# One expert's second weights and w_in change places between attention and the expert stage, and hash bits are written by one instruction and transfers

## The chip, the cores and the metric

The kernel runs on one core of a Trainium2 chip. The metric is the device time of one execution in microseconds. Before the change it is 560.36 us, the median of three runs (559.76 to 561.38). All figures of the profile come from one more execution that was profiled.

## The reference

Three layers follow each other, on float32 inputs of 2 x 8 heads x 768 tokens x 64:

```python
# 1. attention between tokens of the same hash
q_bits = (einsum(q, proj) > 0); k_bits = (einsum(k, proj) > 0)     # 6 bits each
mask = bucket(q_bits)[:, None] == bucket(k_bits)[None, :]
attn = softmax(where(mask, q @ k.T / 8, -1e9)) @ v                 # -> x, 1536 x 512
# 2. mixture of 8 experts, each token to the one of its largest logit
e = argmax(x @ w_gate)
x = gate * sigmoid(x @ w_output_gate)[e] * (relu(x @ w1[e]) @ w2[e])   # 512 -> 1024 -> 512
# 3. h = x @ w_in (512 -> 1024); solu = h * softmax(h); layer norm; @ w_out (1024 -> 512)
```

w_in and w_out come as 64-bit floats, all else as 32-bit.

## The kernel before

**Numbers in halves.** TensorE multiplies 16-bit floats. A 32-bit matrix is split into a high half (the value rounded to 16 bits) and a low half (the rest), and three products (high-high, high-low, low-high) are added. So every weight has to be loaded, scaled, rounded (`w_hi`, L141, on ScalarE) and subtracted (`w_lo`, L144, on VectorE), or split by three POOL instructions (`w_split`, L179). An expert's w1 or w2 comes in four loads of 512 KB (`w_load`, L152) into tiles of the pool `raw`, which has five buffers, used in turn: a new tile waits until the one five places earlier has been read. w_in and w_out, being 64 bits wide, come in eight pieces each of 128 x 512 values (`wide_load`, L101) into five buffers `raww`. A piece is decoded to 32-bit floats: ScalarE takes Abs of its upper word (L122), VectorE shifts and joins the words in three steps (L123, L125, L126; `wide_a`) and sets small values to zero in a fourth (L131; `wide_b`), and then `w_hi` and `w_lo` split it.

**Attention** (`attention`, L281) works on 96 units: eight pairs of heads, two blocks of queries, two heads, three tiles of 128 queries. The loop over units (L938) issues for unit i: the scores of 128 queries against 768 keys (`emit_s`, L530, four products), between them the transposes of unit i-2's probabilities (L577), the row maximum on VectorE (L548), the exponential on ScalarE (L563), a part of the product with v, and what was put into a list for this unit by `at(i, f, ...)`. That list, written out by hand (L874 to L906), is where all other work is placed: splitting and transposing the next pair's q and k, hash bits, the routing of tokens to experts, the zero fill of the row buffer xs (`zero`, L273), and the loads and POOL splits of w1 and w2 of experts 0 and 1 (`pieces`, L902: 16 loads). Twelve units, one pair of heads, are called a period here; its units are counted from 0.

The mask is not applied but added: the operands `c` and `b` hold the hash bits as large values, and the second product of `emit_s` adds them to the scores. A product (`bits_mm`, L489) gives the sums whose signs are the bits, four groups of 32 rows for two heads and two halves of the tokens, in one PSUM tile; `bits_rows` (L506) compares one group of 32 rows x 384 columns and writes it to 32 other rows of `c` or `b`. So there are four VectorE instructions for q and four for k in each of seven periods, spread over units 5, 6, 9, 10 and 11 of the period ahead (`BITS`, L874).

Every engine runs its instructions in the order in which they are issued. SyncE's queue carries nearly all transfers, in one order too: a transfer whose tile is not free holds those behind it.

**The seam** (L961 to L1160) ends attention, routes the last tokens, sorts the experts by their token counts and starts the expert stage. Three wide pieces are loaded there, then `x_load(1)` (L1033), a transposing transfer of the rows of the second expert, which waits until all tokens are scattered to xs, then the next weights and two more pieces.

**The expert stage** is a list of 64 slots (L1165), four for each expert's first layer (`mm1`) and four for its second (`mm2`), in the order m1 0, m1 1, m2 0, m1 2, m2 1, m1 3, ... m2 6, m2 7. A slot holds 24 products. `prep` (L1166) says which weight load is rounded in which slot (its low half follows in the next, its load goes out three slots ahead); slots 4 to 47 and 52 to 55 have one. `WD` (L1186) gives the slot in which the decoding of each of the 16 wide pieces begins. After an `mm2` pair, ScalarE writes the high half of yT and VectorE the low half (L1145, L1146); the latter is issued a slot later (`run_late`) and frees the PSUM buffer, one of four that both layers take in turn.

The last stage multiplies by w_in (L1260), applies the activation and the norm, and multiplies by w_out (L1325).

Of the kernel before, what the change touches and what calls it, by code (L numbers as in the profile page):

```python
# [21 lines left out]
def kernel(  # L22
# [77 lines left out]

    def wide_load(x, dec, t=None):  # L101
        if t is None:
            t = dec.tile([128, 512, 2], I32, tag="raww", name="raww", bufs=5)
# [11 lines left out]
    def wide_a(x, dec):  # L115

        t = wide_t.pop(x)
        hi, lo = t[:, :, 1], t[:, :, 0]
        d = nc.vector
        b = dec.tile([128, 512], I32, tag="db", name="db")  # L120
        m = dec.tile([128, 512], F32, tag="dm", name="dm", bufs=1)
        nc.scalar.activation(out=m, in_=hi, func=AF.Abs)  # L122
        d.tensor_scalar(out=b, in0=hi, scalar1=0x07FFFFFF, scalar2=3, op0=ALU.bitwise_and,  # L123
                        op1=ALU.logical_shift_left)
        d.scalar_tensor_tensor(out=b, in0=lo, scalar=29, in1=b, op0=ALU.logical_shift_right, op1=ALU.bitwise_or)  # L125
        d.scalar_tensor_tensor(out=b, in0=hi, scalar=-0x40000000, in1=b, op0=ALU.bitwise_and, op1=ALU.bitwise_or)  # L126
        dec_t[x] = b.bitcast(F32), m
# [12 lines left out]

    def w_hi(src, dst, c0, scale):  # L141
# [6 lines left out]
    wt = {}  # L148
    rawq = {}
# [17 lines left out]
    def w_args(name, e, c):  # L167
# [6 lines left out]
        if c == 0 and (name, e) not in wt:  # L174
            tag = "wb" if name == "w2" else "wa"
            wt[name, e] = wp.tile([128, 2, 4096], F16, tag=tag, name=tag)
# [104 lines left out]
    def attention(es):  # L281
# [232 lines left out]
        bt_ = {}  # L514
# [353 lines left out]
        def gather_copy():  # L868
            xw = raw.tile([128, 1024], F32, tag="raw", name="raw").bitcast(F16)[:, 0:8 * CAP]
            xw = gx["xw"] = xw.rearrange("p (c n) -> p c n", c=8)  # L870
            for kk in range(4):
                nc.scalar.copy(out=xw[:, kk::4], in_=gx["ps"][kk][:, 0:2 * CAP].rearrange("p (a n) -> p a n", a=2))

        BITS = (((5, "q"), (0, 1)), ((6, "q"), (2, 3)),  # L874
                ((9, "k"), (0,)), ((10, "k"), (1, 2)), ((11, "k"), (3,)))
        for n in range(1, NP):
# [8 lines left out]
            for x, gs in BITS:  # L885
                at(s0 + x[0], bits, n, x[1], gs)
# [13 lines left out]
        for e in range(E):  # L900
            at(8 + 4 * e, zero, e)
        pieces = [(nm, e, c) for e in range(2) for nm in ("w1", "w2") for c in range(4)]  # L902
        for x, pc in enumerate(pieces):
            s0 = 12 * (x // 2) + ((10 if x % 2 else 4) if x < 14 else (5 if x % 2 else 1))
# [19 lines left out]
    with tc.manual_schedule():  # L924
# [90 lines left out]
        PRE = 5 if wide else 0  # L1015
        if wide:
# [361 lines left out]
```

## Time and profile before

| | |
|---|---|
| time of the profiled execution | 559.89 us |
| its span, first to last instruction | 558.0 us |
| TensorE (PE) busy | 516.1 us, 92% |
| VectorE (DVE) busy | 422.0 us, 76% |
| ScalarE (ACT) busy | 341.1 us, 61% |
| POOL busy | 260.2 us, 47% |
| mean granted TensorE clock | 0.995 |
| moved by DMA | 81.74 MB |

The stages, from the starts of their first matmuls: attention 9.43 to some 254, the seam to 267.69, the expert stage to 422.28, the last stage to 558.0. Slot 24 of the expert stage begins at 331.27, slot 32 at 351.07, slot 40 at 373.91, slot 48 at 392.84.

Of the rows below, a timeline row gives the start, the length, the engine ("SPq" is SyncE's queue), the line, the operation, the tiles written and read, their sizes, and in brackets the idle time before it and what ended it. A row of a group by lines gives the count, the total busy time and the mean length in ns. A waits row gives the total, the number and the longest. A windows row gives start and end, the length, each engine's busy time and instructions (PE, PEld for TensorE's weight loads, DVE, ACT, POOL), the granted TensorE clock, the DMA engines' busy share and the GB/s moved; length less busy time is idle time.

### The profile page before, as it was taken

How to read it: one execution, taken by the hardware profiler on the slowest of the kernel's cores; microseconds unless marked ns; L12 is line 12 of the kernel's file. 1: busy time of each engine (PE TensorE's matmuls, PEld its weight loads, DVE VectorE, ACT ScalarE, POOL GpSimd, SP SyncE). 2: the span in 40 equal slices, each digit the busy share in tenths (PEclk: the TensorE clock that was granted, in tenths of full speed). 3: DMA queues.
4: the chain of work that ended last, by engine and by line, in shares of the span. 5: the costliest groups of instructions: out<-in, count | busy, mean ns of one | idle time of the engine just before them, and what ended most of it. 6: DMA issues, size and time to landing. Idle time of an engine off the chain costs nothing. (4 is left out here: it accounts for less than half of the span.)

```text
span 558.0 us, 10766 instructions
## 1 busy us (share of the span) xinstructions
PE 516.1 (92%) x3900; PEld 348.8 (63%) x3900; DVE 422.0 (76%) x935; ACT 341.1 (61%) x642; POOL 260.2 (47%) x324
## 2 busy tenths in 40 slices
PE   6799999999899999999997988968999999999994
PEld 5455656656555555667997988968995444444441
DVE  7877878788888898757699899889981875455540
ACT  6678687777767777764376776776661554244240
POOL 7959483838587674625247556331330111111112
PEclk9999999999999999999999999989999999999999
DMA  5576758453819166003687999999700252423442
GB/s 169 113 227 106 252 87 273 85 175 62 256 32 220 67 137 174 2 1 117 220 239 172 282 286 275 236 336 303 264 4 2 38 95 58 113 56 66 105 82 70
DMA packets 104488, 81.74 MB, mean 146 GB/s; under 512 B 79728, under 2 KB 86768, under 8 KB 104432
## 3 DMA queue, kind: packets, MB, share of 16 engines
q1 hardware_dynamic: 102128, 74.71, 51.8%
q0 software_dynamic: 2304, 6.31, 3.1%
q8 instruction: 32, 0.52, 0.4%
q14 instruction: 24, 0.20, 0.1%
HBM read 51.43 MB, written 9.97 MB: 110 GB/s over the span
## 5 line engine op out<-in xcount | busy, mean ns | idle before, releaser
L563 ACT ACTIVATE p<-s,mx 128x768 f32<-128x768 f32 x96 | 95.2, 992 | 56.3 <-DVE mx L552 46.9
L577 PE MATMUL t<-ident,p 128*128 128x128 f32 x576 | 125.4, 274 | 0.9 <-ACT pt L579 0.6
L548 DVE TENSOR_REDUCE mx<-s 128x1 f32<-128x768 f32 x96 | 91.6, 954 | 24.2 <-PE s L538 21.6
L579 ACT COPY pt<-t 128x384 f32<-128x384 f32 x192 | 84.5, 478 | 10.1 <-PE t L577 8.8
L577 PEld LDWEIGHTS t<-ident,p 128*128 128x128 f32 x576 | 78.0, 141 | 15.9 <-ACT pt L579 7.0
L596 PE MATMUL v<-pt,v 128*64 128x384 f32 (+1 forms) x384 | 80.1, 503 | 2.9 <-DVE xt L623 2.5
L1116 POOL TENSOR_TENSOR hh<-hf,hh 128x448 f16<-128x448 f32 (+5 forms) x32 | 42.9, 1346 | 79.6 <-ACT hf L1115 70.4
L1105 PE MATMUL a<-xw,wa 128*128 128x224 f16 (+5 forms) x224 | 55.8, 253 | 15.9 <-DVE yT L1146 14.8
L1325 PE MATMUL o<-wo,zT 128*128 128x512 f16 x288 | 64.0, 379 | 2.1 <-DMA zT<-z 2.1
L1260 PE MATMUL h<-wi,yT 128*128 128x512 f16 x288 | 64.0, 380 | 1.2 <-ACTq L1065 0.6
L1136 PE MATMUL a<-hh,wb 128*128 128x224 f16 (+5 forms) x256 | 63.5, 251 | 0.0
L1137 PE MATMUL a<-hh,wb 128*128 128x224 f16 (+5 forms) x256 | 63.5, 251 | 0.0
L1138 PE MATMUL a<-hh,wb 128*128 128x224 f16 (+5 forms) x256 | 63.5, 251 | 0.0
L538 PE MATMUL s<-k,q 128*128 128x384 f16 x192 | 58.7, 330 | 4.0 <-ACT p L563 4.0
L538 PE MATMUL s<-b,cm 128*128 128x384 f16 x192 | 57.3, 326 | 1.1 <-DVE b L510 1.1
L1107 PE MATMUL a<-xw,wa 128*128 128x224 f16 (+5 forms) x224 | 55.9, 253 | 1.5 <-DVE wa L146 1.5
L1106 PE MATMUL a<-xw,wa 128*128 128x224 f16 (+5 forms) x224 | 55.9, 253 | 0.0
L1325 PEld LDWEIGHTS <-zT 128*128 128x128 f16 x288 | 27.9, 98 | 36.8 <-DMA zT<-z 3.6
L1260 PEld LDWEIGHTS <-yT 128*128 128x128 f16 x288 | 27.9, 98 | 35.7 <-issue 0.9
L538 PEld LDWEIGHTS <-q 128*128 128x128 f16 x192 | 19.4, 101 | 39.5 <-issue 37.7
L1275 ACT ACTIVATE ex<-h,st,csc 128x1024 f32<-128x1024 f32 x12 | 14.4, 1203 | 45.8 <-DVE st L1298 34.5
L1272 DVE TENSOR_REDUCE st<-h 128x1 f32<-128x1024 f32 x12 | 14.7, 1224 | 31.9 <-PE h L1260 31.9
(256 smaller groups left out, 1038.4 us busy)
## 6 DMA issues: line engine op xcount, KB each, us to landing
raw<-in_moe_w_dram SPq DMA_DIRECT2D x64, 512.0 KB, 6.2
raww<-in_moe_w_in_dram SPq DMA_DIRECT2D x8, 512.0 KB, 8.2
raww<-in_moe_w_out_dram SPq DMA_DIRECT2D x8, 512.0 KB, 6.2
xs<-raw SPq DMA_DIRECT2D x8, 448.0 KB, 6.9
v<-in_v_dram SPq DMA_DIRECT2D x8, 384.0 KB, 5.5
q<-in_q_dram SPq DMA_DIRECT2D x7, 384.0 KB, 4.7
k<-in_k_dram SPq DMA_DIRECT2D x7, 384.0 KB, 5.8
cm<-q SPq DMA_DIRECT2D x14, 96.0 KB, 2.1
```

What stands on the lines that cost most here:

```text
L538: nc.tensor.matmul(t[:, c, 0:SB], d[x, h][:, s], flat(d[y, h])[:, c * SB:(c + 1) * SB], start=first, stop=not first)
L548: nc.vector.tensor_reduce(out=mx[:, 0:1], in_=t[:, :, 0:SB], op=ALU.max, axis=AX.XY)
L563: nc.scalar.activation(out=p, in_=s_t.pop(i)[:, :, 0:SB], func=AF.Exp, scale=mx[:, 1:2], bias=mx[:, 2:3], accum_out=sums[j][:, qt, h:h + 1])
L577: nc.tensor.transpose(t[:, g * 128:(g + 1) * 128], p[:, c, g * 128:(g + 1) * 128], ident)
L579: nc.scalar.copy(out=pt[j, h][:, 3 * c:3 * c + 3, qt * 128:(qt + 1) * 128], in_=t[:, 0:SB].rearrange("p (g c) -> p g c", g=3))
L596: nc.tensor.matmul(pv[j, q0][64 * h:64 * h + 64, 0:w], vt[:, h, c], pt[j, h][:, c, q0 * 128:q1 * 128], start=(c == 0), stop=(c == NS - 1), ...
L1106: nc.tensor.matmul(ps[:, i, 0:n], w[:, 0, kk, fs], xw[:, KD + kk], start=False, stop=False)
L1136: nc.tensor.matmul(ps, w[:, 0, f, ds], hh[:, 0, f], start=(f == 0), stop=False)
L1137: nc.tensor.matmul(ps, w[:, 0, f, ds], hh[:, 1, f], start=False, stop=False)
L1138: nc.tensor.matmul(ps, w[:, 1, f, ds], hh[:, 0, f], start=False, stop=(f == KF - 1))
L1260: nc.tensor.matmul(ps[:, c], yT[:, a, kk, ts], w_i[:, w, kk, c * 512:(c + 1) * 512], start=(kk == 0 and a == 0 and w == 0), stop=(kk == KD ...
L1325: nc.tensor.matmul(ps, zT[:, KF * a + f], w_o[:, w, f], start=(f == 0 and a == 0 and w == 0), stop=(f == KF - 1 and a == 1))
```

## The change

Three things change.

Pieces of w_in (eight) are loaded and decoded during attention into the tile `wi`, one piece every 11 units from unit 6 on: load four units ahead into a `raw` tile, Abs and the first VectorE step in unit u, the other three in u+1 to u+3, `w_hi` on ScalarE in u+4, and the low half on POOL in u+5 (two instructions, `wide_lo_pool`). In their place w2 of expert 1 is no longer loaded and split in attention: `pieces` has 12 loads instead of 16. Its tile now lies in the pool `yp`, which begins after attention.

At the seam, w2 of expert 1 is loaded (two loads ahead of `x_load(1)`, the others behind) and split in slots 0 to 4 by ScalarE and VectorE. Of the wide pieces only the eight of w_out are left for the expert stage; `WD` begins them in slots 2, 5, 8, 11, 14, 20, 26 and 32.

Hash bits of a pair: one VectorE instruction on 128 partitions writes all four groups into a `raw` tile, and four transfers on SyncE's queue take the groups to their rows; units 5 and 9 of the period hold them. The zero fill of xs goes out in units 9 to 16 instead of every fourth unit from 8 to 36.

```diff
@@ wide_a, now in three steps, with raw tiles when dec is None
-        t = wide_t.pop(x)
+        for step in range(3):
+            wide_s(x, dec, step)
+    def wide_s(x, dec, step):
+        t = wide_t[x]
...
+            if dec is None:
+                bm = raw_t()
+                b, m = bm[:, 0:512], bm[:, 512:1024].bitcast(F32)
...
+    def wide_lo_pool(x):
+        src, dst, c0, scale = wide_parts(x)
+        hi, lo = (dst[:, a, c0:c0 + 512] for a in range(2))
+        nc.gpsimd.tensor_scalar(out=src, in0=src, scalar1=scale, scalar2=1.0, op0=ALU.mult, op1=ALU.mult)
+        nc.gpsimd.tensor_tensor(out=lo, in0=src, in1=hi, op=ALU.subtract)
@@ attention
-        def bits(n, which, gs):
-            if 0 in gs:
-                bt_[n, which] = ps_m.tile([128, 512], F32, tag="m", name="m")
-                bits_mm(n, which, range(4), bt_[n, which])
-            for g in gs:
-                bits_rows(n, which, g, bt_[n, which])
+        def bits(n, which):
+            m = ps_m.tile([128, 512], F32, tag="m", name="m")
+            bits_mm(n, which, range(4), m)
+            x, i, val, cmp = ("c", 0, MASK, ALU.is_ge) if which == "q" else ("b", 1, -MASK, ALU.is_le)
+            t = raw.tile([128, 1024], F32, tag="raw", name="raw").bitcast(F16)[:, 0:SB]
+            nc.vector.tensor_scalar(out=t, in0=m[:, 0:SB], scalar1=thr[:, i:i + 1], scalar2=val, op0=cmp, op1=ALU.mult)
+            for g in range(4):
+                h, blk = divmod(g, 2)
+                r = slice(64 - 64 * h, 96 - 64 * h)
+                nc.sync.dma_start(out=flat(op[n][x, h])[r, blk * SB:(blk + 1) * SB], in_=t[32 * g:32 * g + 32])
...
-        BITS = (((5, "q"), (0, 1)), ((6, "q"), (2, 3)),
-                ((9, "k"), (0,)), ((10, "k"), (1, 2)), ((11, "k"), (3,)))
+        BITS = ((5, "q"), (9, "k"))
...
-            at(8 + 4 * e, zero, e)
-        pieces = [(nm, e, c) for e in range(2) for nm in ("w1", "w2") for c in range(4)]
+            at(9 + e, zero, e)
+        pieces = [(nm, e, c) for nm, e in (("w1", 0), ("w2", 0), ("w1", 1)) for c in range(4)]
+        wt["wi", 0] = wp.tile([128, 2, 4096], F16, tag="wi", name="wi", bufs=1)
+        for x in range(2 * KD if wide else 0):
+            u = 6 + 11 * x
+            at(u - 4, wide_load, x, None)
+            for step in range(3):
+                at(u + step, wide_s, x, None, step)
+            at(u + 3, wide_b, x)
+            at(u + 4, lambda x: w_hi(*wide_parts(x)), x)
+            at(u + 5, wide_lo_pool, x)
@@ seam and expert stage
+        for c in range(2):
+            w_load("w2", 1, c)
         x_load(1, slice(NT, NT + CAP))
...
-        prep = [None] * 4
+        prep = [("w2", 1, c) for c in range(4)]
...
-        WD = [0, 2, 4, 6, 8] + [14 + 4 * x for x in range(11)]
+        WD = [2, 5, 8, 11, 14, 20, 26, 32]
...
-        for x in range(4, 4 + LA):
-            if prep[x]:
-                w_load(*prep[x])
+        for x in range(2, LA):
+            w_load(*prep[x])
+        expert(2)
```

## Rows read from the trace of the kernel before

**Rows 1.** Windows: three kinds of attention period, and the expert stage in two parts.

```profile
98.53:128.55 30.02, 29.90 (x206) 18.09 (x205) 24.21 (x57) 22.73 (x49) 19.41 (x23) 1.00 0.49 121
128.55:160.26 31.71, 30.00 (x210) 18.18 (x209) 26.86 (x71) 22.80 (x49) 23.18 (x29) 1.00 0.53 140
160.26:192.30 32.04, 30.19 (x210) 18.27 (x208) 27.65 (x71) 22.61 (x49) 22.85 (x28) 1.00 0.57 139
192.30:222.78 30.48, 30.39 (x207) 18.07 (x205) 27.49 (x71) 22.84 (x53) 19.32 (x22) 1.00 0.59 142
...
267.69:331.27 63.58, 55.70 (x577) 54.64 (x577) 56.61 (x99) 41.78 (x73) 31.57 (x30) 1.00 0.83 236
331.27:392.84 61.57, 52.11 (x578) 51.14 (x577) 56.32 (x63) 43.23 (x67) 23.03 (x21) 0.97 1.02 286
```

**Rows 2.** Windows: the expert stage by eight slots, from slot 24 on.

```profile
331.27:351.07 19.80, 17.75 (x194) 17.45 (x193) 19.15 (x21) 13.78 (x21) 11.06 (x12) 1.00 1.12 264
351.07:373.91 22.84, 18.20 (x194) 17.81 (x193) 18.38 (x23) 15.48 (x25) 5.91 (x5) 0.93 0.97 288
373.91:392.84 18.93, 16.16 (x195) 15.87 (x193) 18.79 (x21) 13.97 (x23) 6.05 (x6) 1.00 0.96 308
```

**Rows 3.** Waits of TensorE, 267 to 393 us.

```profile
PE a L1105 <- DVE yT L1146: 14.8, 9, 4.6
```

**Rows 4.** Groups by line of VectorE, 267 to 408 us.

```profile
L146 DVE SCALAR_TENSOR_TENSOR wb<-raw,wb 128x1024 f16<-128x1024 f32 x22 | 32.5, 1482 | 0.0
L146 DVE SCALAR_TENSOR_TENSOR wa<-raw,wa 128x1024 f16<-128x1024 f32 x24 | 30.0, 1249 | 0.0
L126 DVE SCALAR_TENSOR_TENSOR db<-raww,db 128x512 int32<-128x512 int32 x15 | 13.1, 872 | 0.5
...
L123 DVE TENSOR_SCALAR db<-raww 128x512 int32<-128x512 int32 x15 | 8.6, 570 | 10.9 <-DMA raww<-in_moe_w_out_dram 4.8 <-issue 3.3 <-DMA raww<-in_moe_w_in_dram 2.8
...
L146 DVE SCALAR_TENSOR_TENSOR wo<-db,g,wo 128x512 f16<-128x512 f32 x7 | 7.8, 1116 | 0.0
```

**Rows 5.** Timeline of VectorE in the expert stage.

```profile
276.33 0.43 DVE L123 TENSOR_SCALAR db<-raww 128x512 int32<-128x512 int32 x1 [3.25 <-issue]
...
280.91 0.69 DVE L125 SCALAR_TENSOR_TENSOR db<-raww,db 128x512 int32<-128x512 int32 x1
...
328.42 0.62 DVE L1146 SCALAR_TENSOR_TENSOR yT<-a,yT 128x448 f32 x1
```

**Rows 6.** Waits of SyncE's queue, whole span.

```profile
SPq L1035 <- DMA xs<-xh,slot_all: 8.0, 1, 8.0
```

**Rows 7.** Groups by line of ScalarE, 267 to 408 us.

```profile
L122 ACT ACTIVATE dm<-raww 128x512 f32<-128x512 int32 x15 | 10.2, 678 | 9.5 <-DMA raww<-in_moe_w_in_dram 3.5 <-DMA raww<-in_moe_w_out_dram 3.2 <-issue 2.7
```

**Rows 8.** Timeline of VectorE and POOL in attention, around 149 us.

```profile
148.55 2.13 POOL L184 TENSOR_TENSOR wa<-raw,wa 128x1024 f16<-128x1024 f32 x1
...
149.03 0.17 DVE L745 TENSOR_REDUCE hn<-oh_all 128x8 f16<-128x24 f16 x1
...
149.23 1.47 DVE L746 TENSOR_TENSOR hs<-hs,hn 128x8 f16<-128x8 f16 x1
```

**Rows 9.** Windows: two attention units, the first a period's unit 1, the second its unit 0.

```profile
70.72:73.16 2.44, 2.43 (x17) 1.33 (x15) 1.71 (x4) 2.19 (x6) 2.36 (x3) 1.00 0.18 36
160.26:162.47 2.21, 2.21 (x17) 1.33 (x15) 2.08 (x5) 1.32 (x4) 2.04 (x5) 1.00 0.00 0
```

**Rows 10.** Timeline: key bits of a pair, and the product that reads them first.

```profile
64.28 0.61 DVE L510 TENSOR_SCALAR b<-m,thr 32x384 f16<-32x384 f32 x1 [0.45 <-PE m L504]
...
69.07 0.33 PE L538 MATMUL s<-b,cm 128*128 128x384 f16 x1
```

**Rows 11.** DMA issues by line: KB each, median us to landing.

```profile
raw<-in_moe_w_dram SPq DMA_DIRECT2D x64, 512.0 KB, 6.2
...
cm<-q SPq DMA_DIRECT2D x14, 96.0 KB, 2.1
```

**Rows 12.** Timeline of SyncE's queue: an issue that waits for nothing.

```profile
181.97 0.47 SPq L158 DMA_DIRECT2D raw<-in_moe_w_dram  x1
```

More of the change, by code (lines that the diff above doesn't have):

```diff
@@ L99, with raw_t @@
     wide_t = {}
+    def raw_t():
+        return raw.tile([128, 1024], F32, tag="raw", name="raw").bitcast(I32)
     def wide_load(x, dec, t=None):
-        if t is None:
+        if dec is None:
+            t = raw_t().rearrange("p (c t) -> p c t", t=2)
+        elif t is None:
             t = dec.tile([128, 512, 2], I32, tag="raww", name="raww", bufs=5)
@@ L115, in wide_a @@
     def wide_a(x, dec):
-        t = wide_t.pop(x)
+        for step in range(3):
+            wide_s(x, dec, step)
+    def wide_s(x, dec, step):
+        t = wide_t[x]
         hi, lo = t[:, :, 1], t[:, :, 0]
         d = nc.vector
[L120 to L127, printed above, removed]
+        if step == 0:
+            if dec is None:
+                bm = raw_t()
+                b, m = bm[:, 0:512], bm[:, 512:1024].bitcast(F32)
+            else:
+                b = dec.tile([128, 512], I32, tag="db", name="db")
+                m = dec.tile([128, 512], F32, tag="dm", name="dm", bufs=1)
+            dec_t[x] = b.bitcast(F32), m
+            nc.scalar.activation(out=m, in_=hi, func=AF.Abs)
+            d.tensor_scalar(out=b, in0=hi, scalar1=0x07FFFFFF, scalar2=3, op0=ALU.bitwise_and,
+                            op1=ALU.logical_shift_left)
+            return
+        b = dec_t[x][0].bitcast(I32)
+        if step == 1:
+            d.scalar_tensor_tensor(out=b, in0=lo, scalar=29, in1=b, op0=ALU.logical_shift_right, op1=ALU.bitwise_or)
+        else:
+            d.scalar_tensor_tensor(out=b, in0=hi, scalar=-0x40000000, in1=b, op0=ALU.bitwise_and, op1=ALU.bitwise_or)
     def wide_b(x):
@@ L148 @@
     wt = {}
+    w2p = [wp, None]
     rawq = {}
@@ L174, in w_args @@
         if c == 0 and (name, e) not in wt:
-            tag = "wb" if name == "w2" else "wa"
-            wt[name, e] = wp.tile([128, 2, 4096], F16, tag=tag, name=tag)
+            if name == "w1":
+                wt[name, e] = wp.tile([128, 2, 4096], F16, tag="wa", name="wa")
+            else:
+                wt[name, e] = (w2p[e % 2] or wp).tile([128, 2, 4096], F16, tag=f"wb{e % 2}", name="wb", bufs=1)
         return [(t, wt[name, e], c * 1024, W_S)]
@@ L884, in attention @@
                 at(s0 + 20, load, n + 1, "v")
-            for x, gs in BITS:
-                at(s0 + x[0], bits, n, x[1], gs)
+            for x, which in BITS:
+                at(s0 + x, bits, n, which)
         for j in range(2 * NP):
@@ L1026 @@
         mp = moe.enter_context(tc.tile_pool(name="mp", bufs=2, reuse_waits="tile"))
-        for nm in ("wi", "wo"):
-            wt[nm, 0] = yp.tile([128, 2, 4096], F16, name=nm)
+        w2p[1] = yp
+        wt["wo", 0] = yp.tile([128, 2, 4096], F16, name="wo")
         yT = yp.tile([128, 2, KD, NT + CAP], F16, name="yT")
@@ L1184, in each @@
                 f(*a)
-        WD = [0, 2, 4, 6, 8] + [14 + 4 * x for x in range(11)]
-        for x in range(16):
-            i = WD[x] if wide else 3 + 3 * x
+        WD = [2, 5, 8, 11, 14, 20, 26, 32]
+        for x in range(W0 if wide else 0, 16):
+            i = WD[x - W0] if wide else 3 + 3 * x
             if wide:
-                if x >= PRE:
+                if x >= W0 + PRE:
                     put(i - 3, wide_load, x, dec)
@@ L1210 @@
                 each(w_lo, prep[i - 1])
-            if 4 <= i < len(prep) - LA and prep[i + LA]:
+            if i < len(prep) - LA and prep[i + LA]:
                 w_load(*prep[i + LA])
```

13 lines of the change are left out of this document (6 added, 7 removed).

## The prediction

> **What bounds the kernel now.** I read the page first: it gives TensorE 92% of the span and VectorE 76%, so on the average TensorE bounds. The average hides where it does not, so next came the windows by stage, with TensorE's idle time as length less busy time. In attention a period of 12 units (one head pair) lasts 30.0 us with TensorE busy 29.9 [rows 1]: TensorE sets its pace, and VectorE (24.2 us) and ScalarE (22.7 us) fit beside it. The expert stage, 267.69 to 422.28, is different: TensorE is idle 7.9 us up to 331.27 and 9.5 us from there to 392.84, while VectorE is busy 56 us in each half [rows 1]. Cut by eight matmul slots (four of a second layer, four of a first), VectorE works 19.15 of 19.80 us and 18.79 of 18.93 us; in the stretch between, with 18.38 of 22.84 us, it had to wait for loads itself [rows 2]. The waits say who is late: TensorE waits 14.8 us for yT of L1146, the low half that VectorE writes and that frees a PSUM buffer, and next to nothing else [rows 3]. So the expert stage runs at VectorE's pace, with DMA close behind (286 GB/s at a busy share of 1.02) [rows 1].
>
> In the third view, the groups by line, VectorE's work there is: low halves of the expert weights at 1.25 us (w1) and 1.48 us (w2), and per w_in or w_out piece four decoding steps of 0.57, 0.75, 0.87 and 0.85 us (the first and the third stand for the four) and 1.12 us for the low half of w_out [rows 4], 4.2 us for one of 16 pieces.
>
> **The change part by part.**
>
> *Expert stage from 331.27 to 392.84 (slots 24 to 47).* Before, about six pieces were decoded there; in the changed order, with a piece begun at slots 2, 5, 8, 11, 14, 20, 26 and 32, only the pieces of 26 and 32 and the end of that of 20 remain. VectorE then needs 12 x 1.48 + 12 x 1.25 + 6 x 0.6 (yT) + 2 x 4.2 + 1.1 = 45.8 us, where it was busy 56.3. TensorE needs 50.5 us: 52.1 busy less the 1.6 (0.07 x 22.84) that a mean granted clock of 0.93 of the full 2.4 GHz cost in the stretch that also holds its longest wait, 4.6 us [rows 1 to 3]. So VectorE is no longer last, and what comes last is TensorE or DMA. DMA moved 0.286 x 61.6 = 17.6 MB; about five and a half loads of 512 KB go, leaving 14.7 MB, at 286 GB/s 51.4 us. TensorE's bound would return 11.1 us; loads come in bursts behind the transposes of x, so I leave 2.0 us for waits on DMA and take 9.1 us, with 6 and 11.1 as ends.
>
> *Expert stage up to 331.27.* VectorE cannot start before 276.33 (3.25 us of register loads end there, which stay) [rows 5]. The yT write whose end lets TensorE go on is that of slot 20; it ended at 328.42 + 0.62 = 329.04 [rows 5]. In the changed order VectorE has to do up to there: 8 low halves of w2 x 1.48 = 11.9 (four of them the new w2 at the seam), 12 of w1 x 1.25 = 15.0, five whole pieces x 4.2 = 21.0, the first three steps of the sixth 2.2, three yT 1.9: 52.0, so 328.3. The w2 that came in weighs what the two or three pieces that went out weigh, and I cost this part at 0. Its bounds: -2 us (the 2.8 us of waits for w_in loads before 331 go too) to +3 us (steps that meet a subtract of POOL: their mean of 0.87 us holds 0.69 alone and longer ones beside it [rows 4, 5], and a fifth of the 16 to 20 steps lengthened by 0.8 us are 3).
>
> *Loads at the seam.* SyncE's queue stood for 8.0 us before the transposed load of x, which needs the scattered rows [rows 6]. Two of w2's four loads now go ahead of it, in that gap; the other two and the last w_out loads follow. Cost 0; x for the second expert is behind 1 MB more, which at 286 GB/s takes 3.7 of those 8.0 us. If that cover failed, slot 4 would wait by those 3.7 us.
>
> *Decoding in attention.* Eight pieces, each four VectorE steps in four successive units, one ScalarE Abs of 0.68 us [rows 7] and one ScalarE conversion of the same size, and on POOL a scaling and a subtract of 512 columns; POOL loses four w2 splits, whose subtract alone is 2.13 us for 1024 columns [rows 8], and gains eight scalings and subtracts of half that width, so it is not the bound. A VectorE step that meets nothing takes 0.43 (the first) or 0.69 us [rows 5]: 2.5 us a piece, 20 us in all. But in attention POOL is busy 19 to 23 of 30 us [rows 1]. What a meeting does there is shown at 149 us: a VectorE add of 8 columns, 1.47 us long, ended just when POOL's 2.13 us subtract ended; the reduction before it, begun inside the same subtract, took 0.17 [rows 8]. I put 0.35 us on each of the 32 steps, half of a POOL instruction of some 1.1 us times the 0.65 of the time that POOL is busy: 11 us. So VectorE gains 31 us. It loses 42 of the 56 bit-row instructions at 0.61 us, 25.6 us [rows 10]; the 14 new ones on 128 partitions have the same 384 columns and the same PSUM source, and cost 0.6 each.
>
> What VectorE's extra time costs TensorE is read from the three periods that hold the routing: VectorE +2.65, +3.45 and +3.3 us over its 24.2, length +1.7, +2.0 and +0.5 over 30.0 [rows 1]: 4.2 of 9.4, or 0.45. Net VectorE +5.4 us would cost 2.5 us; if the bit rows were hidden and their removal returned nothing, 31 x 0.45 = 14 us. Below zero there is one place: a unit of 2.44 us follows each set of key-bit rows, where 2.21 is usual [rows 9], 7 x 0.23 = -1.6. ScalarE's 10.9 us more lie beside 7 us of slack a period, though a single 0.68 us can push its copies past the moment when TensorE wants the buffer. I take +4.5, nearer to the low end because the steps are spread one to a unit and the heaviest rows leave the same stretch; ends -1.6 and +14.
>
> *Bits by transfer.* The key bits are ready at 64.28 + 0.61 = 64.9 and first read at 69.07 [rows 10]. Two transfers serve the first head; with 0.47 us an issue [rows 12] and the 2.1 us that a copy of 96 KB takes to land [rows 11], they are there at 67.9. Cost 0 with 1.2 us in hand. Were a copy stuck behind a weight load (6.2 us to landing [rows 11]), it would come 2.9 us late, seven times: 20 us.
>
> *The earlier zero fill* and the shorter POOL queue I cost at 0: nothing waits for the fill before the first scatter, which comes after the routing of the first tokens.
>
> One rule of the Trainium skill speaks against the change. The rows at 149 us [rows 8] show who is blocked: the add with two SBUF inputs, not the reduction with one. The page "SBUF — State Buffer", section "Who interferes with whom", says the same in general: a VectorE instruction with two SBUF inputs, or in a 2-port mode, and a GpSimd instruction that reads SBUF take one port pair for their whole length, and the second blocks. The trace agrees in these rows. By it all 32 new steps contend, and the 42 bit rows that go, with a PSUM source, never did; it makes the first rival below likelier.
>
> Sum: -9.1 + 0 + 0 + 4.5 + 0 = -4.6 us. The profiled execution took 559.89 us (558.0 span and 1.9 around it), 0.5 under the median of 560.36; 559.9 - 4.6 = 555.3 there, 555.8 at the median. I forecast 555.5 us.
>
> **The rivals.**
>
> *Port contention makes attention pay more than the experts return.* Place: the units with a decoding step, worst those with the output steps of a block and those of 160 to 175 us, where the routing is. Price: 31 us at 0.45 with nothing back for the bit rows, 14 us; 559.9 - 9.1 + 14 = 564.8. It decides from 9.1 us on. For it: the two first periods with routing lost 0.6 us for each us that VectorE was given, and held the blocked add [rows 1, 8]. Against it: later units absorbed routing steps nearly free (+0.5 for +3.3).
>
> *Attention takes it for nothing.* The steps fill what the bit rows leave, the -1.6 comes in full or part, and the experts reach TensorE's pace: 559.9 - 11.1 + 0 = 548.8, down to 547.2. For it: VectorE's total there rises only 5.4 us in 250. Against it: the steps fall in other units than the bit rows did.
>
> *DMA or the crowded first slots keep the expert stage.* Five pieces and a w2 in the first 17 slots cost 3 us more, or the loads hold the second half at 6 us of gain: 559.9 - 6 + 4.5 = 558.4, with both 561.4. For it: share 1.02 already [rows 1]. Against it: 2.9 MB less.
>
> *The bits land late*: 20 us, 575.
>
> **How the numbers follow.** Forecast 0.43 (552 to 558); attention for nothing 0.22 (547 to 552); DMA or first slots 0.18 (557.5 to 561.5); contention 0.14 (562 to 568); late bits 0.03. The range 547 to 562 leaves out the last two and little else. A difference of 0.3%, 1.7 us, is what measurements of this kernel can tell from none; faster is below 558.7: 0.43 + 0.22 + 0.06 = 0.71. Same, to 562.0: 0.12 of the third and 0.01 of the fourth, 0.13. Slower 0.16.
>
> **What would show it.** In the profile after: TensorE's idle time between slots 24 and 47 falls from 9.5 to about 2 us and its waits on L1146 there go; those up to slot 23 stay near 8. A period of attention with a decoding piece lasts 30 to 31 us. VectorE steps of decoding show lengths of 0.69 us and of 1 to 2 us beside POOL. No wait of TensorE for a transfer of bits. Wrong if the periods grow by over 1.2 us each, or if TensorE's idle time after slot 24 stays above 6 us with ScalarE waiting for weight loads.

## The result and the profile after

565.7 us, the median of four runs (564.5 to 568.77), beside 560.06 for the kernel before: a ratio of 1.0116 with an interval of 1.0092 to 1.0139. The forecast was 555.5 and its range ended at 562. The profiled execution took 564.85 us, its span is 563.0 us, 5.0 more than before. The stages, from the starts of their first matmuls:

| stretch | before, us | after, us | difference | predicted |
|---|---|---|---|---|
| attention and seam, to the start of slot 0 | 258.26 | 268.61 | +10.35 | +4.5 |
| slots 0 to 23 | 63.58 | 66.63 | +3.05 | 0 |
| slots 24 to 47 | 61.57 | 52.79 | -8.78 | -9.1 |
| the rest | 165.2 | 165.6 | +0.4 | 0 |

The gain is there as forecast; the costs are three times as large (13.4 us against 4.5). The windows of these stages, columns as in [rows 1], the kernel after:

```profile
9.44:278.05 268.61, 249.80 (x1725) 154.00 (x1723) 205.84 (x526) 193.14 (x412) 173.43 (x232) 0.99 0.54 141
...
278.05:344.68 66.63, 57.47 (x577) 55.85 (x577) 58.92 (x99) 44.45 (x74) 36.36 (x30) 0.97 0.93 247
344.68:397.47 52.79, 50.24 (x579) 49.94 (x577) 43.60 (x44) 40.02 (x62) 25.16 (x21) 1.00 1.03 297
```

And the first of these stretches in the kernel before:

```profile
9.43:267.69 258.26, 246.55 (x1726) 152.51 (x1724) 209.21 (x536) 185.06 (x396) 170.02 (x228) 1.00 0.51 133
```

Compare the two: VectorE is busy 3.4 us *less* in attention, yet attention is 10.35 us longer. TensorE's idle time grew by 7.1 us (11.7 to 18.8) and its busy time by 3.25. The busy time grew because the clock fell: in the windows below of the kernel after the granted clock is 0.50, the lower level of 1.2 GHz.

```profile
31.00:34.00 3.00, 3.00 (x11) 1.36 (x12) 2.13 (x5) 2.71 (x6) 0.68 (x1) 0.50 0.82 249
208.30:211.30 3.00, 3.00 (x13) 2.13 (x11) 2.04 (x5) 1.31 (x3) 1.02 (x2) 0.50 0.70 133
341.30:344.30 3.00, 3.00 (x19) 2.54 (x18) 2.62 (x3) 1.66 (x3) 1.26 (x1) 0.50 0.91 91
```

The trace's clock records put these stretches at 30.6 to 34.0, 208.1 to 211.5 and 341.2 to 344.6 us; half of 3.4 us, 1.7, is the most that each can cost. Each follows an idle time of TensorE: 1.36 and 0.60, 1.94, and 4.52 us. (The kernel before has one up to slot 48, in the 0.97 of [rows 1].)

These falls of the clock are not fixed by the kernel. e5_wd and e12_early_load below have the same attention, instruction for instruction; their slot 0 begins at 276.91 and 278.06. In e5_wd TensorE idled as long in units 8 and 74 (1.37 and 0.60 us, 1.94 us) and longer in unit 24, but the clock stayed at 1.00 all through attention. TensorE in e5_wd, and the windows behind these waits:

```profile
73.84 0.32 PE L569 MATMUL s<-b,cm 128*128 128x384 f16 x1 [2.75 <-DMA b<-raw]
...
206.59 0.87 PE L627 MATMUL v<-pt,v 128*64 128x384 f32 x4 [1.94 <-DVE xt L654]
...
73.90:77.30 3.40, 3.40 (x24) 2.09 (x23) 1.88 (x4) 2.23 (x5) 3.23 (x4) 1.00 0.87 286
206.70:210.10 3.40, 3.40 (x24) 2.28 (x24) 2.83 (x9) 1.85 (x4) 0.50 (x2) 1.00 0.76 146
```

So single places of one attention differ between executions by up to 1.6 us, and a difference of that size between two runs below is no proof.

**Where attention lost it.** Cut by single units, the loss does not lie in all periods:

| units | longer than before, us | the same in e5_wd |
|---|---|---|
| 7 to 9 | 1.94 | 1.01 |
| 19, 20 | 1.0 | 0.74 |
| 24 | 1.66 | 2.92 |
| 74, 75 | 4.08 | 2.45 |
| 52 and 89 | 0.87, 0.77 | 0.87, 0.77 |
| 56 | -0.99 | -0.99 |
| unit 1 of five periods | -0.23 each | -0.23 each |
| all others together | about 2.2, none over 0.7 | about 2.6 |

Where the pieces of units 28, 39, 50 and 61 are decoded, attention is 0.5 to 1.3 us longer for each. Units 7 to 9: timelines of the kernel after, VectorE, then POOL, ScalarE and TensorE.

```profile
27.85 1.54 DVE L138 TENSOR_SCALAR raw<-raw 128x512 int32<-128x512 int32 x1 [0.53 <-DMA raw<-in_moe_w_in_dram]
29.32 0.94 DVE L579 TENSOR_REDUCE mx<-s 128x1 f32<-128x768 f32 x1
...
26.99 2.13 POOL L212 TENSOR_TENSOR wa<-raw,wa 128x1024 f16<-128x1024 f32 x1
...
28.40 0.65 ACT L137 ACTIVATE raw<-raw 128x512 f32<-128x512 int32 x1
28.95 0.85 ACT L610 COPY pt<-t 128x384 f32<-128x384 f32 x2
...
28.55 0.32 PE L569 MATMUL s<-k,q 128*128 128x384 f16 x1 [1.36 <-ACT p L594]
29.48 0.33 PE L608 MATMUL t<-ident,p 128*128 128x128 f32 x1 [0.60 <-ACT pt L610]
```

The first decoding step (L138, 0.43 us when alone) first waited for its load and then ended 0.3 us after POOL's subtraction. Behind it stood the row maximum (L579). But TensorE's 1.36 us is not the step's doing: TensorE waited for an exponential that began at 27.42, before the step, and e14_bits_clean, which has no pieces of w_in in attention, shows the same 1.36 us in this place (before: 1.07). The 0.60 us is a wait for the copy pt, behind ScalarE's Abs; e1_no_decode, which keeps the Abs and has no steps, shows it too. In units 7 to 9 that run lost 0.4 us and e5_wd, with the steps and the full clock, 1.0: so the steps cost some 0.6 us here, and 0.9 of the 1.94 goes with the half clock. Units 74 and 75, VectorE, POOL and TensorE of the kernel after:

```profile
204.84 1.35 DVE L143 SCALAR_TENSOR_TENSOR raw<-raw 128x512 int32<-128x512 int32 x1
206.11 0.54 DVE L654 COPY xt<-v 128x384 f32<-128x384 f32 x1
...
204.74 2.23 POOL L368 TENSOR_TENSOR kl<-k,ks 128x384 f16<-128x384 f32 x2
...
206.71 0.87 PE L627 MATMUL v<-pt,v 128*64 128x384 f32 x4 [1.94 <-DVE xt L654]
```

Here the copy that frees the PSUM buffer v stood behind a step that ran beside POOL's subtractions of k and took 1.35 us instead of 0.68; TensorE waited 1.94 us, and in this execution half clock followed. Unit 24, SyncE's queue and TensorE: the key bits were issued at 69.80, and TensorE waited for them.

```profile
69.80 2.41 SPq L552 DMA_DIRECT2D b<-raw  x4
...
73.80 0.32 PE L569 MATMUL s<-b,cm 128*128 128x384 f16 x1 [1.50 <-DMA b<-raw]
```

**Slots 0 to 23.** Slot 22 is 3.5 us longer than before and slot 23, at half clock, 1.6; the other slots are 2.1 us shorter together. SyncE's queue, then VectorE:

```profile
330.77 0.47 SPq L115 DMA_DIRECT2D raww<-in_moe_w_out_dram  x1
...
338.38 0.43 DVE L138 TENSOR_SCALAR db<-raww 128x512 int32<-128x512 int32 x1 [2.30 <-DMA raww<-in_moe_w_out_dram]
...
340.18 0.61 DVE L1186 SCALAR_TENSOR_TENSOR yT<-a,yT 128x448 f32 x1
```

A w_out load took 7.6 us, VectorE stood 2.30 us for it, and yT, which frees a PSUM buffer, was behind; TensorE then idled 4.52 us. The waits of TensorE from 267 to 398 us (total, times, longest), to be held against [rows 3]:

```profile
PE a L1145 <- DVE yT L1186: 8.9, 4, 4.5
...
PE a L1176 <- DVE yT L1186: 1.4, 1, 1.4
```

### The profile page after: what moved, and what is told of

The parts are those of the page before. It is cut to its first block, busy times and chain, and to the rows that moved or that the text cites. A ratio compares the mean times of both kernels' runs of the same rounds, so it can differ in the third digit from the quotient of the medians.

```text
span 563.0 us, 10833 instructions
## 1 busy us (share of the span) xinstructions
PE 519.6 (92%) x3900; PEld 350.5 (62%) x3900; DVE 394.9 (70%) x889; ACT 344.6 (61%) x646; POOL 269.7 (48%) x328
## 5 line engine op out<-in xcount | busy, mean ns | idle before, releaser
L579 DVE TENSOR_REDUCE mx<-s 128x1 f32<-128x768 f32 x96 | 91.5, 953 | 39.1 <-PE s L569 37.3
L610 ACT COPY pt<-t 128x384 f32<-128x384 f32 x192 | 84.3, 480 | 12.5 <-PE t L608 11.7
L1156 POOL TENSOR_TENSOR hh<-hf,hh 128x448 f16<-128x448 f32 (+5 forms) x32 | 45.8, 1433 | 64.2 <-ACT hf L1155 63.9
L170 DVE SCALAR_TENSOR_TENSOR wb<-raw,wb 128x1024 f16<-128x1024 f32 x28 | 39.6, 1424 | 9.6 <-ACT wb L166 9.5
```

What stands on the lines that cost most here:

```text
L579: nc.vector.tensor_reduce(out=mx[:, 0:1], in_=t[:, :, 0:SB], op=ALU.max, axis=AX.XY)
L610: nc.scalar.copy(out=pt[j, h][:, 3 * c:3 * c + 3, qt * 128:(qt + 1) * 128], in_=t[:, 0:SB].rearrange("p (g c) -> p g c", g=3))
```

## The experiments

Four questions: what decoding costs, what the bits are worth, whether place or POOL makes the loss, and what held slots 0 to 23. Times stand with the ratio to the kernel before, run beside them, and its interval; windows and waits are those of one profiled execution. The diffs are shortened; remarks behind # do not stand in the kernels.

**e1_no_decode**, the steps left out:

```diff
-            for step in range(3):
-                at(u + step, wide_s, x, None, step)
-            at(u + 3, wide_b, x)
+            at(u, wide_s, x, None, 0)     # Abs, and a POOL memset for the four steps
```

> The changed kernel without the four VectorE steps that decode a piece of w_in in attention (32 instructions left out, a POOL memset of the piece in their place, so w_in is not decoded); loads, Abs, high and low halves stay. Attention grew by 10.4 us. Theory A (a few meetings: the steps hold up the copy xt or a row maximum in units 7 to 9, 19, 52 and 74, and TensorE falls to half clock for 3.4 us after two of these idles): about 8 us come back, all but the late bits, 565.7 to about 557.5. Theory B (each step pays for port contention, spread over all pieces): the same 8 us here, but e4 tells them apart. Theory C (the bits by transfer and the zero fill are what costs): at most 2 us come back, over 563.

558.82 us, 0.9976 (0.9949 to 1.0003). Slot 0 began at 271.20 instead of 278.05, although units 24 and 25 lost 3.76 us to late key bits and the half clock that followed. So the steps are most of the cost: without them and those 3.76 us attention is 0.3 us shorter than before.

**e2_old_bits**:

```diff
-        BITS = ((5, "q"), (9, "k"))
+        BITS = (((5, "q"), (0, 1)), ((6, "q"), (2, 3)),
+                ((9, "k"), (0,)), ((10, "k"), (1, 2)), ((11, "k"), (3,)))
```

> The changed kernel with the old bit rows (four VectorE instructions a set, no transfers, spread over units 5, 6, 9, 10, 11). Theory A: the wait of 1.5 us for a bit transfer in unit 24 goes, but 0.22 us in unit 1 of each period come back and VectorE has 25 us more beside the decoding: 564 to 568. Theory C: 560 or less, attention 8 us shorter.

575.44 us, 1.0255 (1.0207 to 1.0304). Slower than any theory had it: beside the decoding, the 25 us of bit rows are worth 9.7 us. The transfers are not what made attention longer.

**e3_zero_spread**, the zero fill from rows of cm that are zero, spread out again:

```diff
-            at(9 + e, zero, e)
+            at(8 + 4 * e, zero, e)
```

> The changed kernel with the zero fill again every fourth unit from 8 to 36, read from rows that are zero anyway, so that it needs no raw buffer. Theory A: the transposes of the third pair are no longer late (they were issued 7 us later than before), the key bits of unit 24 land in time, and 1.7 to 2.5 us come back: about 563.5. Theory B and a theory that bit transfers are late by themselves: under 0.7 us.

565.84 us, 1.0106 (1.0068 to 1.0144). Unit 24 lost 0.32 us instead of 1.66 (2.92 and 1.9 in e5_wd and e12_early_load, which have the fill of after); units 74 and 75 still lost 4.0, and slots 0 to 23 took 66.41 us with half clock twice. The mechanism holds for unit 24; the expected time was not reached, and that slot 0 began 1.3 us earlier (276.72) shows nothing, as in e5_wd it begins 1.1 us earlier without this edit.

**e4_units**:

```diff
-            u = 6 + 11 * x
+            u = (9, 21, 33, 45, 57, 69, 81, 87)[x]
```

> The changed kernel with the pieces begun in units 9, 21, 33, 45, 57, 69, 81 and 87 instead of 6 + 11 x: the four steps then lie in units 3 to 5 and 0 of each half period (and never in the unit ahead of the copy xt or in that of the output steps), and not with the routing of units 72 to 75; the same steps, the same POOL work beside them. Theory A: units 7 to 9 lose their 2.0 us, 19 its 0.8, 74 and 75 their 4.1, and half of that comes back elsewhere: 560 to 562. Theory B: within 1.5 us of 565.7.

568.45 us, 1.0156 (1.011 to 1.0202). The expectation was missed by its sign. But unit 11 alone lost 6.39 us; all else of the change was better than in after by 3.4. SyncE's queue, VectorE and TensorE there:

```profile
34.70 4.36 SPq L552 DMA_DIRECT2D b<-raw  x4
...
39.76 0.43 DVE L138 TENSOR_SCALAR raw<-raw 128x512 int32<-128x512 int32 x1 [5.09 <-DMA b<-raw]
...
40.83 0.47 PE L608 MATMUL t<-ident,p 128*128 128x128 f32 x1 [4.35 <-ACT pt L610]
```

The step waited, at the head of VectorE's queue, for the transfers of the key bits: they still read a tile of `raw`, from whose five buffers the step's own tile comes. (The expectation of e6_units2 below calls this the piece's load; the row says otherwise.) Six more periods lost 0.6 to 1.2 us in unit 0 or 1, where steps at units 9 to 12 meet POOL's splits (six of them took 2.1 to 2.45 us). In unit 11 half clock followed the idle time, 6.8 us long.

**e5_wd**:

```diff
-        WD = [2, 5, 8, 11, 14, 20, 26, 32]
+        WD = [20, 26, 32, 38, 44, 48, 52, 57]
```

> The kernel after with the eight w_out pieces at slots 20, 26, 32, 38, 44, 48, 52, 57 instead of 2, 5, 8, 11, 14, 20, 26, 32. In the trace of after, slots 0 to 24 took 66.63 us (63.58 before), VectorE was busy for 59 us of them, and the longest TensorE idle (4.52 us at 340.85) stood behind a decoding step that waited 2.30 us for its w_out load. Theory A (VectorE's order in the first 24 slots is the bound, and a step that waits for its load holds yT behind it): slots 0 to 24 in 57 to 61 us, slots 24 to 48 in 53 to 57, the whole about 559 to 562. Rival B (the bound is the sum of VectorE's work and of the loads in the stage, so that the same steps cost the same wherever they stand): slots 0 to 24 shorter, 24 to 48 longer by as much, the whole at 565 to 567. The start of slot 0 stays at 277 to 279 by both.

558.36 us, 0.9962 (0.9932 to 0.9992). Better than theory A. Windows of this kernel, slots 0 to 23 and 24 to 47:

```profile
276.91:333.23 56.32, 55.05 (x577) 54.65 (x577) 38.86 (x74) 38.78 (x64) 33.98 (x30) 1.00 1.02 279
333.23:387.83 54.60, 51.89 (x578) 51.27 (x577) 49.84 (x52) 41.03 (x63) 23.95 (x21) 0.97 1.01 270
```

TensorE is idle 1.3 us in the first 24 slots, 9.2 in after; the two pieces more cost 1.8 us in the next 24. VectorE's work is the same over the whole kernel, its place is not. (The profiled execution took 554.93 us, 3.4 less than the median of the run.)

**e6_units2**, with e3's zero fill:

```diff
-            u = 6 + 11 * x
+            u = (17, 26, 38, 50, 56, 62, 77, 86)[x]
```

> The kernel after with the zero fill of e3_zero_spread and the w_in pieces at units 17, 26, 38, 50, 56, 62, 77, 86 instead of 6, 17, 28, ..., 83. In the traces so far the loss of attention stands in single units, each with a decoding step that met a late load, a long POOL instruction or the routing: units 7 to 9 and 74 to 75 in after (1.94 and 4.08 us), unit 11 in e4_units (6.39 us, VectorE waited 5.09 us for the first piece's load), unit 0 or 1 of each period in e4_units (about 1 us each); pieces that began in units 1 to 5 of a period cost nothing. Theory A (single collisions): without those places slot 0 starts at 269 to 271.5 and the time is 557 to 560. Rival B (POOL's and VectorE's use of the same operands slows both wherever they overlap, so that places only move the loss): slot 0 at 275 to 280, time 563 to 567.

561.25 us, 1.0013 (0.999 to 1.0035); slot 0 at 272.27, so 5.8 us of 10.35 came back by the places of the pieces and of the zero fill. Rival B falls. Theory A was 0.8 us short: the piece at 56 cost 2.3 us in units 59 and 60, beside POOL's splits, and unit 12 lost 1.7 to late key bits.

**e7_both**, the edits of e5_wd and e6_units2:

> e6_units2 and e5_wd together. By theory A of both the gains add: slot 0 at 269 to 271.5, the expert stage 3 to 6 us shorter than in after, about 551 to 555, so faster than the kernel before. By theory B of both 563 to 567. If only the attention theory holds, 557 to 560; if only the one on the slots holds, 559 to 562.

549.62 us, 0.9791 (0.9744 to 0.9838): faster than both kernels. The gains add: the profiled executions of e5_wd, e6_units2 and this kernel are 9.9, 4.1 and 13.5 us below that of after. Slot 0 is at 272.26, as in e6_units2.

**e8_bits**, the kernel before with the new bits and the zero fill of after:

```diff
-        BITS = (((5, "q"), (0, 1)), ((6, "q"), (2, 3)),
-                ((9, "k"), (0,)), ((10, "k"), (1, 2)), ((11, "k"), (3,)))
+        BITS = ((5, "q"), (9, "k"))
...
-            at(8 + 4 * e, zero, e)
+            at(9 + e, zero, e)
```

> The kernel before with one part of the change alone, the hash bits by one instruction and four transfers (and the zero fill at units 9 to 16). It leaves VectorE about 27 us less to do in attention. My prediction set this part at 0 by itself; e2_old_bits (the old bits beside the decoding in attention) was 9.7 us slower than after. Theory A (in attention TensorE sets the length and VectorE has room, so that freed VectorE time is worth something only where more work is put into it): 558.5 to 561, slot 0 at 267 to 269. Rival B (VectorE's work sets attention's length by a part of it anywhere): 27 us less at the ratio of .45 that I used, 548 to 552. Rival C (the transfers come late, as the 1.5 us in unit 24 of after): 561 to 565, with the idle in unit 24 and half clock behind it.

557.6 us, 0.9947 (0.9927 to 0.9966). Slot 0 at 266.50, with 3.56 us lost in unit 24; SyncE's queue and TensorE:

```profile
66.94 2.41 SPq L524 DMA_DIRECT2D b<-raw  x4
...
70.92 0.32 PE L541 MATMUL s<-b,cm 128*128 128x384 f16 x1 [2.17 <-DMA b<-raw]
```

None of the three holds as it stands. Outside unit 24 attention is 4.7 us shorter than before, which A denies and B has at more than twice that; the late transfer of C takes 3.56 us of it back.

**e9_all**, e7_both with three more moves:

```diff
-        BITS = ((5, "q"), (9, "k"))
+        BITS = ((5, "q"), (8, "k"))
...
-            at(8 + 4 * e, zero, e)
+            at((13, 14, 16, 18, 25, 28, 30, 37)[e], zero, e)
...
-            u = (17, 26, 38, 50, 56, 62, 77, 86)[x]
+            u = (17, 28, 39, 50, 61, 76, 82, 88)[x]
```

> e7_both with three more moves, from its trace: the key bits at unit 8 of a period instead of 9 and the zero fill at units 13, 14, 16, 18, 25, 28, 30, 37 (in e7_both the key bits of the second pair were issued over 4.6 us on a queue with two zero fills on it and landed 1.4 us late, with half clock behind: 1.56 us in unit 12), and the w_in pieces at 17, 28, 39, 50, 61, 76, 82, 88 (in e7_both the piece at 56 cost 2.3 us in units 59 and 60, beside POOL's splits; after unit 72 POOL has no more expert weights to split). Theory A (single collisions): slot 0 at 267 to 269.5 instead of 272.26, the time 545 to 548. Rival B (moving collisions makes others): slot 0 at 271 to 274, time 549 to 552.

553.15 us, 0.9882 (0.9856 to 0.9908); slot 0 at 275.50. Worse than B has it: the ninth unit of six periods lost 0.4 to 2.1 us (the tenth got 0.7 back). In the first of them TensorE waited 0.80 us until the bits' VectorE instruction had read the PSUM tile m, which the routing's product writes next. (The expectation lays half clock to unit 12 of e7_both; the clock there stayed at 1.00, TensorE waited 1.40 us for the bits.)

**e10_bits_early**, e8_bits with the first two of these moves:

> The kernel before with the new hash bits alone, as e8_bits, but with the zero fill at units 13 to 37 and the key bits at unit 8. In e8_bits slot 0 began 1.2 us earlier than in before; 3.56 us of a late key-bit transfer in unit 24 hid a gain of 4.8 us in the rest of attention. Theory A (the transfers are late only because SP's queue is crowded there): no idle for the bits, slot 0 at 262 to 264, time 552 to 555.5. Rival B (a transfer in this place is late by itself): the idle comes back in some unit, time 556.5 to 559.

566.05 us, 1.0127 (1.01 to 1.0155). The same loss in the ninth unit, 1.1 to 1.5 us in five periods, and 1.76 in unit 24. In unit 24 TensorE waited 1.60 us for a transfer of bits again, as B has it; but slot 0 (269.78) and the time fit neither, as the earlier bits brought a cost of their own. The zero fill, too, is read from cm here.

**e11_no_sub**:

```diff
-        nc.gpsimd.tensor_tensor(out=lo, in0=t, in1=hi, op=ALU.subtract)
+        nc.gpsimd.memset(lo, 0.0)      # so too in the splits of q and k
```

> The kernel after without POOL's subtractions in the splits of q, k and the expert weights in attention (a memset of the low halves stands in their place, so the low parts are left out of the result). Everything that VectorE does and every transfer stays. In after, eight of the twelve w_in steps in units 0 to 95 that took 1.0 to 2.0 us instead of .42 or .68 ended within .5 us of the end of such a subtraction. Theory A (a decoding step that meets POOL's long operation is held until it ends, and what stands behind it on VectorE is late): the steps take .42 and .68 us, units 7 to 9 and 74 to 75 lose under 1 us each instead of 1.94 and 4.08, slot 0 at 271 to 274.5. Rival B (the loss there comes of the order on VectorE and of loads, not of POOL): the same units lose 1.5 and 3 us or more, slot 0 at 276 to 279.

562.53 us, 1.0063 (1.0038 to 1.0088); slot 0 at 274.87 although units 24 and 25 lost 3.9 us to the key bits. All other units lost 3.2 us instead of 8.9. Of these 5.7 us, 1.6 are a half clock in units 74 and 75 that e5_wd does not have either, with the subtractions in place; so POOL's subtractions are worth some 4 us, mostly in units 19, 28, 52 to 54 and 61. VectorE in the two places above, and TensorE in unit 74:

```profile
27.64 0.43 DVE L138 TENSOR_SCALAR raw<-raw 128x512 int32<-128x512 int32 x1 [0.63 <-DMA raw<-in_moe_w_in_dram]
...
203.27 0.68 DVE L143 SCALAR_TENSOR_TENSOR raw<-raw 128x512 int32<-128x512 int32 x1
203.87 0.55 DVE L654 COPY xt<-v 128x384 f32<-128x384 f32 x1
...
204.48 0.87 PE L627 MATMUL v<-pt,v 128*64 128x384 f32 x4 [1.51 <-DVE xt L654]
```

These steps have their own length (five of the 32 still run over, by 2.8 us, beside POOL's other work). Units 74 and 75 lost 1.85 us, without half clock; TensorE's wait there is 1.51 us instead of 1.94, so POOL's hold is 0.4 of it and the order on VectorE the rest. Units 7 to 9 still lost 1.93, with the same two idle times (1.36 and 0.59 us) and half clock again. So A fails in both places that it names; its part lies elsewhere.

**e12_early_load**:

```diff
-                    put(i - 3, wide_load, x, dec)
+                    put(i - 8, wide_load, x, dec)
```

> The kernel after with the last three w_out pieces' loads issued eight slots ahead of their decoding instead of three. In after the load for slot 20's step was issued at 330.77, landed at 338.36, and VectorE waited 2.30 us for it with yT queued behind (TensorE idle 4.52 us, then half clock for 3.4 us). Theory A (that late load is the +3.05 us of slots 0 to 24): 61 to 64 us for slots 0 to 24, the time 561 to 563.5. Rival B (slots 0 to 24 are longer since the loads of the second expert's w2 and what follows crowd the queues, so another wait takes its place): slots 0 to 24 at 65.5 or more, time 564.5 to 567.

563.74 us, 1.0062 (1.0044 to 1.008). Windows of slots 0 to 23 and 24 to 47:

```profile
278.06:340.62 62.56, 55.95 (x576) 54.71 (x576) 57.91 (x98) 43.74 (x73) 34.99 (x30) 1.00 0.95 265
340.62:396.88 56.26, 51.90 (x579) 51.40 (x578) 47.09 (x46) 41.21 (x63) 25.94 (x22) 0.97 1.03 283
```

The first 24 slots are 4.1 us shorter than in after, a little below before's 63.58, so the late load was the +3.05. (TensorE still waited 2.10 us for yT in slot 22, instead of 4.52.) But 3.5 us of it went in the next 24, where TensorE idled 3.25 us for yT at 377.4 and half clock followed.

**e13_best**, e7_both with two moves:

```diff
-            at(8 + 4 * e, zero, e)
+            at((13, 16, 20, 24, 28, 32, 36, 40)[e], zero, e)
...
-            u = (17, 26, 38, 50, 56, 62, 77, 86)[x]
+            u = (17, 28, 39, 50, 61, 76, 82, 88)[x]
```

> e7_both with the zero fill at units 13, 16, 20, 24, 28, 32, 36, 40 and the w_in pieces at 17, 28, 39, 50, 61, 76, 82, 88, the key bits at unit 9 again. In e9_all the key bits at unit 8 cost 1.1 to 2.1 us in the ninth unit of six periods (0.7 came back in the tenth), which hid what its other two moves did. Theory A (single collisions): unit 12 no longer loses 1.56 us nor units 59 and 60 2.3, slot 0 at 268 to 270.5, time 545 to 548.5. Rival B (other units lose as much): slot 0 at 271.5 to 274, time 549 to 552.

550.16 us, 0.9858 (0.9813 to 0.9904), no different from e7_both within the intervals. Units 12, 59 and 60 are clean, slot 0 is at 271.08, but unit 57 lost 1.6 us: B has part of it. That loss is another meeting: VectorE waited for a small copy on POOL, which stood behind the split of an expert weight, and TensorE waited 1.52 us for what VectorE did next. VectorE there, then windows of attention and of slots 0 to 23 and 24 to 47:

```profile
157.43 0.31 DVE L678 TENSOR_REDUCE lg<-lt 128x48 f32<-128x144 f32 x1 [2.49 <-POOL lt L636]
...
9.44:271.08 261.64, 246.53 (x1726) 152.44 (x1724) 202.61 (x526) 192.02 (x412) 170.41 (x231) 1.00 0.58 144
271.08:327.50 56.42, 55.00 (x577) 54.71 (x576) 39.63 (x74) 39.62 (x65) 34.24 (x30) 1.00 1.02 291
327.50:381.23 53.73, 50.24 (x579) 49.95 (x578) 49.01 (x51) 40.06 (x62) 26.17 (x21) 1.00 0.96 263
```

**e14_bits_clean**, e8_bits with the zero fill of e13_best:

> The kernel before with the new hash bits alone and the zero fill at units 13 to 40 as in e13_best, the key bits at unit 9 (in e10_bits_early unit 8 cost 1.3 us a period). Theory A (the wait of 3.56 us in unit 24 of e8_bits comes of SP's queue, which eight zero fills crowd in units 9 to 16): slot 0 at 262.5 to 264.5, time 553 to 556. Rival B (the transfers are late there with any zero fill): 1.5 us or more in unit 24 or 12, time 556.5 to 560.

555.54 us, 0.9928 (0.9896 to 0.996). Unit 24 lost 0.89 us instead of 3.56, slot 0 is at 264.02: theory A, less a late transfer that is still seen. The new bits, with this zero fill, are worth 3.7 us at slot 0 and some 4 in the time. Attention in this kernel:

```profile
9.43:264.02 254.59, 244.49 (x1726) 152.38 (x1724) 183.34 (x494) 185.86 (x396) 169.29 (x227) 1.00 0.56 140
```

**e15_best_no_decode**, e13_best with the edit of e1_no_decode:

> e13_best without the four VectorE steps of each w_in piece in attention (a memset stands in their place, so w_in is left out of the result). The difference to e13_best is what decoding in attention costs where pieces, loads and zero fill don't collide. If VectorE's work adds at the ratio of .45 that I used (26 us of it, 12 us), slot 0 at 257 to 260; if it costs only at collisions, which e13_best avoids, slot 0 within 2 us of e13_best; the 4.6 us that e6_units2 still lost against before, and the 4.8 us that the new bits freed, say between: 4 to 6 us earlier, 262 to 266, time 540 to 544.

547.14 us, 0.9802 (0.9761 to 0.9843), slot 0 at 266.46. Of the three expectations of slot 0 the middle one holds (4.6 us earlier than in e13_best), though not its time:

```profile
9.43:266.46 257.03, 245.51 (x1726) 152.45 (x1724) 184.25 (x494) 192.26 (x412) 170.43 (x239) 1.00 0.59 146
```

Against e13_best: 18.4 us less on VectorE, 4.6 us less in length, a share of 0.25.

## Why the prediction was wrong, step by step

**Expert stage from 331.27: right.** -8.78 against -9.1, and for the reason given: VectorE fell to 43.6 us (45.8 worked out), TensorE's idle time from 9.5 to 2.55, with DMA at 297 GB/s; of the waits for yT there, one of 2.25 us is left.

**Decoding in attention: the step that failed.** It put +4.5, and +10.35 came. The runs divide the loss at slot 0, by the differences of five kernels:

| part | from | us |
|---|---|---|
| new bits, zero fill spread | before to e14_bits_clean, 267.69 to 264.02 | -3.7 |
| the rest of the pieces (ScalarE, POOL, loads) | to e15_best_no_decode, 266.46 | +2.4 |
| the 32 steps where they meet little | to e13_best, 271.08 | +4.6 |
| steps and transfers that collide | to after, 278.05 (276.91 in e5_wd) | +7.0 (5.8) |

What the prediction had no term for is the last line, and it had the first far too large. It took the cost as a share, 0.45, of VectorE's extra time, with the same share back for the time that went: 31 us made 14, and 25.6 us of bit rows gave 11.5 back. That the pieces did cost 14.0 (the last three lines) is luck: e13_best has the same pieces for 7.0. The new bits gave back 3.7 alone, and 8.8 beside the decoding (slot 0 of e2_old_bits is at 286.89). So neither direction has one share. VectorE's busy time shows it, too: in after it is 3.4 us less than before, not 5.4 more, and attention is longer.

The share was itself read from single waits. In the kernel before, TensorE's idle time in the period from 128.55 us on is 1.71 us [rows 1], and one wait holds 1.70 of it, behind the add that [rows 8] shows:

```profile
151.22 0.86 PE L596 MATMUL v<-pt,v 128*64 128x384 f32 x4 [1.70 <-DVE xt L623]
```

It is the copy xt again, as in units 74 and 75 of after. This wait is gone in e14_bits_clean, where unit 56 is 1.76 us shorter: nearly half of what the new bits are worth.

The meetings with POOL were rarer than the prediction put: 10 of the 32 steps in attention ran over by more than 0.1 us, 6.5 us in all against its 11 us. But a few fell where a row maximum, xt or the next scores stood behind. In after, half clock came on top in two places; e5_wd has the same idle times without it and still lost 9.2 us. The 2.44 against 2.21 of [rows 9] did come back, 0.23 in five of the seven periods, the one term below zero. Of the prediction's own signs, a growth of over 1.2 us a period, it came in three of eight.

The rule of the Trainium skill that the prediction weighed (page "SBUF — State Buffer", section "Who interferes with whom") has one port pair for VectorE and GpSimd, which one of them holds for a whole instruction while the other is blocked. The trace agrees: six of the ten long steps end 0.3 to 0.6 us after a subtraction of POOL that they began in. e11_no_sub, where the steps of units 7 and 74 take 0.43 and 0.68 us, agrees too. By the rule all 32 steps can contend; 10 were lengthened.

**Bits by transfer, and the zero fill, at 0: failed in one pair.** The sum had two transfers at 0.47 us an issue with 1.2 us in hand. An issue took 0.6 us, all four 2.41, and the key bits went out at 69.80, behind the eight zero fills and the transposes that these delayed; e3_zero_spread and e14_bits_clean show that cause. It cost 1.66 us in after, and 2.92 in e5_wd.

**Expert stage up to 331.27, at 0: failed, at its bound of +3.** The bound's reason, steps stretched by POOL, was not it. A w_out load was late and VectorE waited with yT behind it; e12_early_load takes this away and e5_wd avoids it. The seam held: TensorE waits 0.67 us in slot 0 (before 0.71) and not in slot 4.

**The rivals.** The first, contention, had 564.8 us and said that it decides from 9.1 us on; that is where the time went. Its place was partly right (the routing's units 74 and 75), its mechanism half: of 8.9 us without the bits' wait, some 4 go when POOL's subtractions go; the rest is half clock, ScalarE's Abs and the order on VectorE, as far as units 7 to 9 and 74 show. Its flat 0.45 us per us was as wrong as the forecast's, so that its 564.8 us came near the result is luck. The third had 3 us more in the first slots; they came, but by one late load in slot 22 and not by a crowd in the first 17, and they did not keep the second half from its gain. Late bits were foreseen seven times; one was late.

Not settled: why bits are still late in unit 24 of e14_bits_clean (0.9 us), why the median of e10_bits_early (566.05 us) lies 3.5 us above its profiled execution (562.6), which slot 0 at 269.78 nearly explains, and when the clock falls.

## What to carry to other kernels

When work moves under a stage where TensorE sets the pace, don't price it by its share of an engine's time: list, unit by unit, what stands behind each moved instruction in its queue, which load or buffer it waits for, and what long operation of POOL runs then. Here after, e7_both and e13_best do the same work in 565.7, 549.6 and 550.2 us, almost by place alone. Don't credit work that is taken away at the same rate, either: what it returns depends on what stood behind it. And set every decoding step where its load landed long ago: at the head of an in-order queue a late load stops everybody behind.

## What the runs showed of the hardware

A short idle time of TensorE can cost more than itself. After idle times of 1.94 us (unit 74) and of 1.36 and 0.60 (units 7 and 8) the granted clock of after was 0.50 for 3.4 us; in e5_wd it stayed at 1.00 after the same idle times, and after 2.75 us in unit 24. So whether it falls can't be told from the length of one idle time in these runs. Units 74 and 75 lost 4.08 us with the fall and 2.45 without, and units 7 to 9 1.94 and 1.01. This can make gains in one place come back as losses in another (e12_early_load).

The issue of a 24 KB transfer between SBUF tiles took 0.6 us of SyncE's queue, more than the 0.47 of a 512 KB load [rows 12]; four of them in a row took 4.4 us in e4_units, just ahead of the zero fills.
